# A convolution and ELU feed-forward kernel: first tile in token halves, conv output permuted on its way into PSUM

## Chip, cores, metric

The kernel runs on one core of a Trainium2 chip. The metric is the device time of one execution in microseconds (us); lower is better. It is measured over several runs, and one further execution is profiled. Engines are called by their short names: PE (TensorE, matrix multiply; PEld is its weight load), DVE (VectorE), ACT (ScalarE), POOL (GpSimd), SP (SyncE, here only a DMA queue).

## What is computed

```python
def _attn_ref(x, weight):            # x (8, 4096, 192), weight (8, 7)
    w = softmax(weight, axis=-1)     # with 1e-9 added to the sum
    x_pad = np.concatenate([np.zeros((B, 6, 192)), x], axis=1)
    idx = np.arange(S)[:, None] + np.arange(7)[None, :]
    x_unf = x_pad[:, idx, :].reshape(B, S, 7, 8, 24)
    return np.einsum('hk,bskhg->bshg', w, x_unf).reshape(B, S, 192)

def _moe_ref(x, w_in, w_out):        # w_in (192, 2048), w_out (2048, 192)
    h = x @ w_in
    g = np.where(h > 0.0, h, np.exp(np.minimum(h, 0.0)) - 1.0)
    return g @ w_out
```

A causal convolution of seven taps over the sequence, with one set of taps for each of 8 heads of 24 channels, is followed by a feed-forward layer with ELU, over 8 x 4096 = 32768 tokens.

## The kernel before

The tokens are cut into 32 tiles of 1024 (`SUP`), each into two groups of 512 (`GS`). Channels are split into three blocks j of 64; group 0 uses partitions 0 to 63 of every operand and group 1 partitions 64 to 127. So a matmul has 64 rows of the array, and the two row halves work side by side on the two groups.

For a tile in the steady state:

- *conv* (`c`, L978): eight heads, two row halves: 16 matmuls of 240 columns with band matrices `Tm` as weights over windows of x (`xg`), into a PSUM bank that ACT evacuates to `csb` (L745). A DMA transpose (L597, on SP's queue) makes `att` of it, channels on partitions.
- *h* (`h`, L1003): 16 chunks q of 128 hidden units, two groups: three accumulating matmuls (j = 0, 1, 2) of 512 columns fill one PSUM bank, a unit. There are 1024 units in all.
- *ELU* of a unit: ACT takes exp from PSUM into `E` (L749), POOL clamps E to [0, 1] (L702), DVE computes max(E - 1, h) into `gT` (L865). DVE's combine frees the bank.
- *o* (`o`, L1026): 256 matmuls of 192 columns of `gT` and `w_out` for a tile; ACT evacuates to `osb` (L756), SP writes it out.

The order of PE's instructions is made by a planner in the file when the kernel is built. It keeps a clock for each row half, gives each matmul a duration (`MM_H`, `MM_O`, `MM_C`) and each bank a time at which it is free. For the first 16 steps n (one step is chunk q of tile 0) the function `live` picks what is ready first, from modelled ends of the ELU and from the landing times assumed in `LANDS`; the later steps have fixed places (`O_AT`, `CONV_AT`). Eight banks of PSUM are shared by all kinds of result. The order is fixed: at run time PE executes it in sequence and waits on semaphores.

The first tile doesn't go through `xg`, `Tm` and the DMA transpose. Its path:

- SP loads the weights (L1043) and an 8-token halo `xh` (L1047); ACT loads all 1024 tokens in one DMA (L714, 768 KB), token p*8+i on partition p.
- DVE and ACT make the softmax (L769 to L792, exp at L721), PE spreads it (`s`, L904 and L911), DVE copies it to `wcol` (L799) and multiplies it with the identity into seven diagonal matrices `taps` in one instruction (L801). Two rows of matmuls on zeros (`w`, L900, six and four of them by `WARM`) stand before and after `s`.
- ACT casts x into three channel blocks (L724, three instructions), PE transposes them (`t`, L926; the halo at L937), DVE and ACT evacuate to `xT` (L821, L736).
- PE does the convolution with `taps` (`d`, L954): for j = 0 and 1 five taps of 512 columns, DVE the other two taps (L830, L835, L848); for j = 2 seven taps in two halves of 256, evacuated by ACT and DVE (L740, L850).
- The group 1 copy of `w_in` (partitions 64 to 127) is made from the group 0 rows by ACT (L730, chunk columns 0 to 511, and 1024 to 1279 after unit 6), by DVE (L853, columns 512 to 1023) and by an SP DMA (L1066).

POOL first builds `ones`, `ident`, `owner` and `block8` (L653 to L676), then issues in this order: nine loads of `w_in` (L638; three column chunks, one load for each j, because block j of a head is 8 consecutive rows), the first part of `w_out` (L649), x of tile 1 (L618, two loads), two parts of `w_out`, x of tile 2; then it begins with the clamps. SP also writes the band matrices to DRAM and reads them back shifted as `Tm` (L1049, L1058).

The channel order of `att` in the kernel before is head, j, i (j of 3, i of 8). In the steady state it comes from the way a conv matmul reads x: `"p w (j i) -> p j w i"` over a head's 24 channels (L981), written to PSUM in order.

Of the kernel before, what the change touches and what calls it, by code (L numbers as in the profile page):

```python
# [5 lines left out]
ALU = mybir.AluOpType  # L6
# [31 lines left out]
WARM = (6, 1, 4)  # L38
WCOLS = ((0, 4 * FC), (4 * FC, 8 * FC), (8 * FC, 16 * FC))
WOUT = (0, 4, 8, 16)  # L40
HALO = 8
BW = P
ON_DVE = (2, 2, 0)
XL = GS - CW * (NWIN - 1) + PAD
XI = SUP // P
# [7 lines left out]
LATE_Q, COPY_AT = 10, 6  # L53
LIVE, UNTIL = 16, 16
EARLY_O = (4, 8)
LANDS = {"x": {1: 7200.0, 2: 14200.0}, "w_in": 10200.0, "w_out": (3900.0, 8400.0, 11000.0)}
# [3 lines left out]
TURNS = 260.0  # L60
X_AT = ((2, 1, 1), (1, 1, 0))
ZERO_AT = 8
# [3 lines left out]
def bass_lightweight_conv__then__act_elu_kernel(  # L66
# [41 lines left out]
    conv_half = {}  # L108

# [15 lines left out]
    def modelled():  # L125
        return step[0] < UNTIL
# [9 lines left out]

    def h_items(n, r):
        def issue(j):
            take_bank(("h", n, r), r)
            plan.append((clock[r], ("h", n, r, j)))  # L140
            if j == 2:
                freed[bank_of["h", n, r]] = clock[r] + MM_H + HELD["h"]
                if modelled():
                    elu(n, r, clock[r] + MM_H)

        return [(MM_H, lambda j=j: issue(j), None) for j in range(3)]
# [15 lines left out]
    def o_items(k, g, rt, qs, visit, first, final):  # L162
# [4 lines left out]
        def issue(i):  # L167
            q, kb = todo[i]
            take_bank(("a", k, g), rt)
            if modelled():  # L170
                t = NQ * (k // 2) + q
                clock[rt] = max(clock[rt], gt_at[t, g], turned.get((k, g), 0.0) if first and i == 0 else 0.0)
# [42 lines left out]
    def block_items(n, g, rt):  # L215
        k, b = divmod(n - O_AT[g], NB)
        if k < 1:
            q = n - EARLY_O[g]
            if not 0 <= q < NQ:
                return []  # L220
            items = o_items(0, g, rt, range(q, q + 1), 2 * q + rt, True, True)
            return evacuated(items, 0, g) if q == NQ - 1 and rt == 1 else items
        items = o_items(k, g, rt, range(QB * b, QB * (b + 1)), 2 * b + rt, True, True)
        return evacuated(items, k, g) if b == NB - 1 and rt == 1 else items

    def live(last, convs, turns):
        hq = [list(range(last)) for _ in range(2)]
        cq = [list(convs), list(convs)]
        far = float("inf")

        def h_ready(rt):
# [8 lines left out]
            late = rt == 1 and s == 0 and q >= LATE_Q  # L240
            return max(min(freed), att_at[s], LANDS["w_in"] if late else 0.0)

# [10 lines left out]
        def o_ready(rt, g):  # L253
# [5 lines left out]
            t = max(gt_at.get((NQ * (k // 2) + q, g), far) for q in range(q0, q1))  # L259
# [6 lines left out]
        while any(hq) or any(cq) or any(map(any, turns)):  # L266
            best = None
            for rt in range(2):
# [22 lines left out]
            if what[0] == "h":  # L291
                n = hq[rt].pop(0)
                go(h_items(n, rt))
            elif what[0] == "c":
# [7 lines left out]
            else:  # L302
                g = what[1]
                k, q0, q1, visit = turns[rt][g].pop(0)
                go(o_items(k, g, rt, range(q0, q1), visit, True, True))
# [9 lines left out]
    start_up = [("t", j) for j in (0, 3, 1, 2)] + [("d", j) for j in range(3)]  # L315
    for i, (b, what) in enumerate(
        ((0, ("t", 0)), (3, ("t", 3)), (1, ("t", 1)), (2, ("t", 2)))
        + ((4, ("d", 0)), (5, ("d", 1)), (6, ("d", 2)), (7, ("d", 2)))
    ):
        occupant[b], freed[b] = what, i - 10.0  # L320
        bank_of.setdefault(what, b)
    turns = [[[], []], [[], []]]
    for rt in range(2):
        for g in range(2):
            turns[rt][g] += [(0, q, q + 1, 2 * q + rt) for q in range(LIVE - EARLY_O[g])]
    live(LIVE, [(n, m) for n in range(LIVE) for m in conv_steps.get(n, ())], turns)
    for n in range(LIVE, NP):
        step[0] = n
        if n == UNTIL:
            clock[:] = [max(clock)] * 2  # L330
# [33 lines left out]
    pe_order += [("w", 0, WARM[0]), ("s",), ("w", 0, WARM[2])]  # L364
    for what in start_up:
        pe_order.append(what)
# [3 lines left out]
    for at, item in sorted(plan, key=lambda p: p[0]):  # L370
        if item[0] == "h" and item[3] == 2:
# [3 lines left out]
            act_order.append(item[:3])  # L375
        elif item[0] == "c" and item[2:] == (1, HU - 1):
# [18 lines left out]
    x_before = {}  # L395
    for s in range(2, NS):
# [11 lines left out]
    with ExitStack() as stack:  # L408
# [15 lines left out]
        xs = sbuf("xs", [P, XI, D], FP32)  # L424
        xh = sbuf("xh", [HALO, D], FP32)
        xbh = sbuf("xbh", [HALO, 3, 2, HP], BF16)
        xb = sbuf("xb", [P, 3, XI, HP], BF16)
# [16 lines left out]
        part = sbuf("part", [P, 2, GS], FP32)  # L444
# [10 lines left out]
        s_w = [sema(f"s_w{i}") for i in range(6)]  # L455
        s_wc = sema("s_wc")
        s_sel = sema("s_sel")
# [5 lines left out]
        s_xs = sema("s_xs")  # L463
# [17 lines left out]
        s_wd = sema("s_wd")  # L481
        s_wa = sema("s_wa")
        s_band = sema("s_band")
        s_part = sema("s_part")
# [35 lines left out]
        def att_need(s):  # L520
# [4 lines left out]
            ("t", 0): (0, 1),  # L525
            ("t", 1): (1, 0),
            ("t", 2): (2, 0),
            ("t", 3): (0, 2),
            ("d", 0): (0, 3),
            ("d", 1): (0, 4),  # L530
            ("d", 2): (3, 5),
# [7 lines left out]
        def transposed(j):  # L539
            if j == 3:  # L540
                return xT[:, :, 0:HALO], H[:, bank_of["t", 3], 0 : 3 * HALO].rearrange(
                    "p (j c) -> p j c", j=3
                )
            return xT[:, j, HALO : HALO + GS], H[:, bank_of["t", j], :]

        def first_att(j, c0, c1):
            b = bank_of["d", j] + (j == 2 and c0 > 0)
            return att[:, 0, j, c0:c1], H[:, b, c0:c1]
# [52 lines left out]

        @block.gpsimd
        def _gpsimd(g: bass.BassGpSimd):
# [31 lines left out]
            def load_w_in(k):  # L635
                c0, c1 = WCOLS[k]
                for j in range(3):
                    g.dma_start(  # L638
                        w_in[0:HP, j, c0:c1],
                        bass.AP(  # L640
                            tensor=moe_w_in.tensor,
                            offset=8 * j * FF + c0,
                            ap=[[CPH * FF, HEADS], [FF, 8], [1, c1 - c0]],
                        ),
                    ).then_inc(s_w[k], 16)

            def load_w_out(k):
# [3 lines left out]
                ).then_inc(s_w[3 + k], 16)  # L651
# [11 lines left out]
            ).then_inc(s_id)  # L663
            for step in range(2):
# [20 lines left out]
            load_w_in(0)  # L685
            load_w_in(1)
            load_w_in(2)
            load_w_out(0)
            for gr in range(2):
                load_x(1, gr)  # L690
            load_w_out(1)
            load_w_out(2)
            for gr in range(2):
                load_x(2, gr)
# [17 lines left out]
        def _scalar(a):  # L712
            W = Waits(a)
            a.dma_start(  # L714
                xs[:, :, :], x_flat[0:SUP, :].rearrange("(p i) d -> p i d", i=XI)
            ).then_inc(s_xs, 16)
# [5 lines left out]
            W(s_xs, 16)  # L722
            for j in range(3):
                a.activation(  # L724
                    xb[:, j, :, :].rearrange("p i (h e) -> p (i h) e", e=8),
                    xs[:, :, :].rearrange("p i (h j e) -> p j (i h) e", j=3, e=8)[:, j],
                    ACT.Copy,
                ).then_inc(s_cast)
            def upper_half(c0, c1):
                a.activation(  # L730
                    w_in[HP:P, :, c0:c1], w_in[0:HP, :, c0:c1], ACT.Copy
                ).then_inc(s_wa)

            for j in range(1, 3):
                W(s_xt, j + 2)
                a.activation(*transposed(j), ACT.Copy).then_inc(s_fa)  # L736
            W(s_w[0], 48)
            upper_half(*WCOLS[0])
# [369 lines left out]
```

## Time and profile before

| | us |
|---|---|
| median of 3 runs (lowest, highest) | 723.49 (723.15, 723.59) |
| the profiled execution | 722.73 |
| its span, first to last instruction | 720.8 |
| PE, ACT, POOL, DVE busy in the span | 714.6, 678.6, 670.1, 642.8 |
| mean granted TensorE clock | 1.00 |
| period of a tile in the steady state | 21.85 |

Issues of the first 15 us (start, issue length, landing after issue, us):

| DMA | queue | start | length | landing after |
|---|---|---|---|---|
| wq | SP | 0.80 | 0.41 | wait for it ended at 2.24 |
| xs, 768 KB | ACT | 0.81 | 0.38 | 4.6 |
| w_in, nine | POOL | 2.44 to 7.02 | 0.56 to 0.78 | 3.0 for the first, 6.8 for the last |
| band matrices out | SP | 6.12 | 0.37 | 5.5 |
| w_out, first part | POOL | 7.56 | 0.91 | 7.6 |
| x of tile 1, two | POOL | 8.37, 9.24 | 0.96, 0.95 | 8.1, 10.4 |
| w_out, second, third | POOL | 10.09, 10.83 | 0.85, 0.99 | 10.6, 11.9 |
| Tm | SP | 11.63 | 0.35 | 7.0 |
| x of tile 2, two | POOL | 11.70, 12.56 | 0.97, 0.98 | 12.3, 12.7 |

How to read the views used: a timeline row has the start, the length of the merged stretch, the engine, the line, the operation and tiles, shapes, and in brackets the idle time before it with what ended it. A row by stages has a stretch, its length and the busy time of each engine in it with the number of instructions, then the granted clock, the share of DMA time and the bytes moved. Matmuls are pipelined, so their lengths overlap, and the distance of their starts tells the rate.

### The profile page before, as it was taken

The numbers are of one execution on the slowest core, as the hardware profiler recorded it, in microseconds if no ns is written. First come the engines' busy times: TensorE is split into PE (matmuls) and PEld (weight loads), VectorE is DVE, ScalarE is ACT, GpSimd is POOL, SyncE is SP. The second block draws the span as 40 slices with busy tenths as digits, with TensorE's granted clock in tenths as the row PEclk, the third lists the DMA queues.
The fourth block names the chain that finished last, engine by engine and source line by source line (L and its number), as shares of the span: only waits on it lengthen the run. The fifth ranks groups of instructions, "written<-read, shape, count | busy, mean of one in ns | idle before, by whom it ended". The sixth has DMA issues, their size and how long they took to land.

```text
span 720.8 us, 27612 instructions
## 1 busy us (share of the span) xinstructions
PE 714.6 (99%) x11846; PEld 676.0 (94%) x11847; DVE 642.8 (89%) x1048; ACT 678.6 (94%) x1289; POOL 670.1 (93%) x1115
## 2 busy tenths in 40 slices
PE   8999999999999999999999999999999999999998
PEld 4689999999999999999999999999999999999997
DVE  7989898998899988989888989988989989899994
ACT  6999999999999999999999999999999999999994
POOL 9999999999999999999999999999999999999893
PEclk9999999999999999999999999999999999999999
DMA  9655354554254664344553456552535543645212
GB/s 172 92 87 78 64 90 74 95 87 83 54 96 72 88 97 63 73 83 86 87 97 50 84 74 96 86 86 51 96 73 89 94 69 67 92 79 83 71 35 68
DMA packets 132735, 58.75 MB, mean 82 GB/s; under 512 B 98614, under 2 KB 132036, under 8 KB 132612
## 3 DMA queue, kind: packets, MB, share of 16 engines
q1 hardware_dynamic: 88388, 39.32, 23.9%
q0 software_dynamic: 43936, 16.77, 23.1%
q8 instruction: 93, 1.52, 0.9%
q10 hardware_dynamic: 288, 0.88, 0.4%
q14 instruction: 30, 0.25, 0.1%
HBM read 34.63 MB, written 25.46 MB: 83 GB/s over the span
## 4 chain that ended last, share of the span: by engine, by line
PE 95%; POOL 2%; DVE 1%; ACT 1%; issue 0%; DVEq 0%; POOLq 0%
PE H L1026 54%; PE H L1003 38%; PE H L978 3%; DVE gT L865 1%; POOL w_in L638 1%; ACT E L749 1%; POOL xg L618 0%; POOL w_out L649 0%; ACT csb L745 0%; POOL E L702 0%; POOL owner L666 0%; ACT osb L756 0%; DVE osb L856 0%; POOL block L676 0%; POOL ident L655 0%
## 5 line engine op out<-in xcount | busy, mean ns | idle before, releaser
L865 DVE SCALAR_TENSOR_TENSOR gT<-E,H 128x512 f16<-128x512 f32 x1024 | 633.0, 683 | 64.1 <-POOL E L702 62.4
L1026 PE MATMUL H<-w_out,gT 64*128 64x192 f16 x8192 | 682.2, 243 | 0.1
L1003 PE MATMUL H<-att,w_in 64*128 64x512 bf16 x3072 | 680.3, 376 | 0.6 <-DVE gT L865 0.4
L1026 PEld LDWEIGHTS H<-w_out,gT 64*128 64x128 f16 x8192 | 625.9, 94 | 22.3 <-PE H L1026 1.6
L702 POOL TENSOR_SCALAR E<-E 128x512 f32<-128x512 f32 x1024 | 607.6, 615 | 38.4 <-ACT E L749 28.2
L749 ACT ACTIVATE E<-H 128x512 f32<-128x512 f32 x1024 | 593.1, 602 | 26.5 <-PE H L1003 1.6
L1003 PEld LDWEIGHTS H<-att,w_in 64*128 64x128 bf16 x3072 | 275.2, 93 | 7.9 <-issue 1.2
L978 PE MATMUL H<-xg,Tm 64*128 64x240 bf16 x496 | 91.2, 263 | 0.2 <-DVE gT L865 0.2
L745 ACT ACTIVATE csb<-H 112x480 bf16<-112x480 f32 x124 | 70.1, 565 | 0.1
L756 ACT ACTIVATE osb<-H 128x384 f32<-128x384 f32 (+1 forms) x129 | 62.2, 484 | 6.8 <-PE H L1026 6.8
L618 POOL DMA_DIRECT2D xg<-in_x_dram x62 | 55.4, 898 | 0.2 <-issue 0.2
L978 PEld LDWEIGHTS H<-xg,Tm 64*128 64x128 bf16 x496 | 43.7, 94 | 4.7 <-DVE gT L865 1.1
L856 DVE COPY osb<-H 128x192 f32<-128x192 f32 x1 | 0.4, 358 | 7.3 <-PE H L1026 7.3
L900 PE MATMUL H<-zw 128*128 128x512 bf16 x10 | 4.0, 555 | 1.2 <-DVE zw L764 1.2
L638 POOL DMA_DIRECT2D w_in<-in_moe_w_in_dram x9 | 5.2, 617 | 0.0
L724 ACT ACTIVATE xb<-xs 128x512 bf16<-128x512 f32 x3 | 1.7, 622 | 2.4 <-DMA xs<-in_x_dram 2.4
L954 PE MATMUL H<-xT,taps 128*128 128x256 bf16 (+1 forms) x23 | 3.7, 314 | 0.2 <-issue 0.2
L900 PEld LDWEIGHTS H<-zw 128*128 128x128 bf16 x10 | 1.1, 128 | 2.8 <-issue 1.4
L954 PEld LDWEIGHTS H<-xT,taps 128*128 128x128 bf16 x24 | 2.2, 97 | 1.5
L649 POOL DMA_DIRECT2D w_out<-in_moe_w_out_dram x3 | 2.6, 916 | 0.0
L717 ACT ACT_TABLE_LOAD x1 | 1.3, 1283 | 1.2 <-PEq L1093 1.2
L730 ACT ACTIVATE w_in<-w_in 64x1536 bf16<-64x1536 bf16 (+1 forms) x2 | 2.3, 1164 | 0.0
(43 smaller groups left out, 19.9 us busy)
## 6 DMA issues: line engine op xcount, KB each, us to landing
out_dram<-osb SPq DMA_DIRECT2D x126, 192.0 KB, 3.5
xg<-in_x_dram POOLq DMA_DIRECT2D x61, 240.0 KB, 5.0
xs<-in_x_dram ACTq DMA_DIRECT2D x1, 768.0 KB, 4.6
att<-csb SPq DMA_TRANSPOSE x31, 4.6
w_in<-in_moe_w_in_dram POOLq DMA_DIRECT2D x6, 64.0 KB, 3.0
w_in<-in_moe_w_in_dram POOLq DMA_DIRECT2D x3, 128.0 KB, 5.4
w_out<-in_moe_w_out_dram POOLq DMA_DIRECT2D x2, 192.0 KB, 9.1
w_out<-in_moe_w_out_dram POOLq DMA_DIRECT2D x1, 384.0 KB, 11.9
```

Source lines behind the costliest of these rows:

```text
L618: g.dma_start(xg[0:rows, b, 2 * w0 + gr : 2 * w1 : 2, :], src).then_inc(s_x[b][gr], 16)
L638: g.dma_start(w_in[0:HP, j, c0:c1], bass.AP(tensor=moe_w_in.tensor, offset=8 * j * FF + c0, ap=[[CPH * FF, HEADS], [FF, 8], [1, c1 - c0]], ...
L702: g.tensor_scalar(out=E[:, i % NE, :], in0=E[:, i % NE, :], scalar1=1.0, scalar2=0.0, op0=ALU.min, op1=ALU.max,).then_inc(s_clp)
L745: a.activation(*conv_evac(W, m), ACT.Copy).then_inc(s_ce)
L749: a.activation(E[:, i % NE, :], H[:, bank_of[item], :], ACT.Exp).then_inc(s_exp)
L756: a.activation(*out_evac(W, *item[1:]), ACT.Copy).then_inc(s_oev[item[2]])
L865: v.scalar_tensor_tensor(out=gT[:, s % NG3, q, u, :], in0=E[:, i % NE, :], scalar=1.0, in1=H[:, bank_of[item], :], op0=ALU.subtract, op1=A ...
L900: pe.matmul(H[:, bank, :], zw[:, 0:P], zw[:, 0:GS], start=True, stop=True)
L954: ins = pe.matmul(H[:, bank_of[item] + half, c0:c1], taps[:, tap, :], xT[:, j, HALO - PAD + tap + c0 : HALO - PAD + tap + c1], start=(tap ...
L978: ins = pe.matmul(H[:, bank_of["c", m], 256 * q : 256 * q + UC], Tm[rows, h, :], xg[rows, s % NXB, :, CPH * h : CPH * (h + 1)].rearrange(" ...
L1003: ins = pe.matmul(H[:, bank_of[item[:3]], :], w_in[HP * r : HP * (r + 1), j, FC * q : FC * (q + 1)], att[HP * r : HP * (r + 1), s % 2, j, ...
L1026: ins = pe.matmul(acc_of(k, g)[:, D * kb : D * (kb + 1)], gT[HP * rt : HP * (rt + 1), t % NG3, q, g, t0 : t0 + P], w_out[HP * rt : HP * (r ...
```

## The change

It has these parts:

- **Channel order.** `att` gets the order head, i, j: channel 3p + j is on partition p of block j. `w_in` then loads with three consecutive rows for each partition, all three j in one DMA, in four column chunks (`NCH`). A conv matmul reads x in memory order and writes its 240 columns to PSUM at the places that ACT's evacuation reads as before.
- **x of tile 0** comes in four loads of 64 partitions x 4 tokens: half 0 (the first 256 tokens of each group) and half 1, group 0 on SP, group 1 on ACT; the halo is loaded on ACT's queue between its two.
- **First tile in halves.** One cast, three transposes `t` of 256 tokens, three convolutions `d` with all seven taps on PE for half 0; the same for half 1 as `T` (before the first h) and `D` (placed by `JOBS` after two, two and three steps). The DVE part of the convolution is gone. The first 8 steps (`SPLIT`) compute two chunks q of 256 tokens in one bank, six matmuls of 256 columns, half 0 in steps 0 to 3 and half 1 in steps 4 to 7.
- **POOL's order.** The first `w_in` load goes between `ident` and `owner`, w_out's second part ahead of x of tile 1; x of tile 2 is issued before the first clamp through `X2_AT`.
- **Smaller ones.** `taps` is made in seven instructions; the xbh cast stands ahead of `wcol`; four `w` matmuls after `s` become one, behind `t3`; group 1's `w_in` columns 0 to 1023 are copied by DVE; the early o blocks are laid out anew (`BEGUN`, `LATER`), and so are the planner's landing times.

```diff
-WARM = (6, 1, 4)
-WCOLS = ((0, 4 * FC), (4 * FC, 8 * FC), (8 * FC, 16 * FC))
+WARM = (6, 1, 1)
+NCH = 4
+LATE_Q, COPY_AT = 10, 8
+SPLIT = 8
-LATE_Q, COPY_AT = 10, 6
-LIVE, UNTIL = 16, 16
-EARLY_O = (4, 8)
-LANDS = {"x": {1: 7200.0, 2: 14200.0}, "w_in": 10200.0, "w_out": (3900.0, 8400.0, 11000.0)}
+LIVE = 16
+BEGUN = (6, 5)
+LATER = ((16, 18), (16, 18, 20))
+LANDS = {"x": {1: 8400.0, 2: 14000.0}, "w_in": 11500.0, "w_out": (2600.0, 5400.0, 9000.0)}
+JOBS = ((2, ("D", 0, 0)), (2, ("D", 0, 1)), (3, ("D", 1, 2)))
+X2_AT = (0, 0)
...
-    start_up = [("t", j) for j in (0, 3, 1, 2)] + [("d", j) for j in range(3)]
+    start_up = [("t", 3), ("w", 0, WARM[2]), ("t", 0), ("t", 1), ("t", 2)]
+    start_up += [("d", j) for j in range(3)] + [("T", 0), ("T", 1)]
...
+        def load_first(eng, half, gr):
+            eng.dma_start(
+                xs[HP * gr : HP * (gr + 1), XI * half : XI * (half + 1), :].rearrange(
+                    "p i d -> p (i d)"
+                ),
+                bass.AP(
+                    tensor=x_flat.tensor,
+                    offset=(GS * gr + GH * half) * D,
+                    ap=[[XI * D, HP], [1, XI * D]],
+                ),
+            ).then_inc(s_xs[half][gr], 16)
...
             def load_w_in(k):
-                c0, c1 = WCOLS[k]
-                for j in range(3):
-                    g.dma_start(
-                        w_in[0:HP, j, c0:c1],
...
+                c0, c1 = FF // NCH * k, FF // NCH * (k + 1)
+                g.dma_start(
+                    w_in[0:HP, :, c0:c1],
+                    bass.AP(
+                        tensor=moe_w_in.tensor,
+                        offset=c0,
+                        ap=[[3 * FF, HP], [FF, 3], [1, c1 - c0]],
+                    ),
+                ).then_inc(s_w[k], 16)
...
             ).then_inc(s_id)
+            load_w_in(0)
             for step in range(2):
...
-            load_w_in(0)
             load_w_in(1)
             load_w_in(2)
+            load_w_in(3)
             load_w_out(0)
+            load_w_out(1)
             for gr in range(2):
                 load_x(1, gr)
-            load_w_out(1)
             load_w_out(2)
-            for gr in range(2):
-                load_x(2, gr)
...
-            a.dma_start(
-                xs[:, :, :], x_flat[0:SUP, :].rearrange("(p i) d -> p i d", i=XI)
-            ).then_inc(s_xs, 16)
+            load_first(a, 0, 1)
+            a.dma_start(xh[:, :], x_flat[GS - HALO : GS, :]).then_inc(s_xh, 16)
+            load_first(a, 1, 1)
...
+            cast(0)
             for j in range(3):
...
+                a.activation(*first_evac(("t", j)), ACT.Copy).then_inc(s_fa)
+            cast(1)
+            for j in (0, 2):
+                W(s_first, j + 1)
+                a.activation(*first_evac(("d", j)), ACT.Copy).then_inc(s_fa)
...
+            upper_half(0)
+            W(s_first, 2)
+            v.tensor_copy(*first_evac(("d", 1))).then_inc(s_fd)
             for j in range(2):
+                W(s_xt, 5 + j)
+                v.tensor_copy(*first_evac(("T", j))).then_inc(s_fd)
+            upper_half(1)
...
                     ins = pe.matmul(
-                        H[:, bank_of["c", m], 256 * q : 256 * q + UC],
+                        H[:, bank_of["c", m], 256 * q : 256 * q + UC].rearrange(
+                            "p (j w i) -> p w i j", j=3, i=8
+                        ),
                         Tm[rows, h, :],
                         xg[rows, s % NXB, :, CPH * h : CPH * (h + 1)].rearrange(
-                            "p w (j i) -> p j w i", j=3
+                            "p w (i j) -> p w i j", j=3
                         ),
...
...
-            sy.dma_start(xh[:, :], x_flat[GS - HALO : GS, :]).then_inc(s_xh, 16)
-            W(s_tap, 3)
+            for half in range(2):
+                load_first(sy, half, 0)
+            W(s_tap, KSIZE + 2)
```

## The prediction

> **What bounds the kernel now.** I read the stages first (busy time of each engine per stretch), then the timeline of the first 20 us, then the conv rows, then the groups of instructions. Stages; columns are stretch, length, busy us of PE, PEld, DVE, ACT, POOL, granted clock, DMA share, GB/s:
>
> ```profile
> 15.00:20.00 5.00, 4.88 (x41) 2.50 (x43) 5.00 (x9) 4.95 (x10) 4.79 (x9) 1.00 1.40 244
> 20.00:25.00 5.00, 5.00 (x65) 3.43 (x61) 5.00 (x9) 4.88 (x11) 4.58 (x9) 1.00 1.13 135
> 60.00:80.00 20.00, 20.00 (x341) 19.39 (x338) 18.64 (x31) 19.22 (x38) 18.95 (x33) 1.00 0.57 88
> ```
>
> From 60 us on PE is never idle and the other engines are: the steady state is PE's. Before that, PE's matmuls come sparsely and DVE, ACT and POOL are full. By starts, 15 to 40 us holds 110 matmuls of L1003, 140 of L1026, 24 of L978; at 216, 82.5 and 102.5 ns each (512, 192 and 240 columns at their spacing) and two row halves side by side that is 11.9+5.8+1.2 = 18.9 us of work in 25: 6.1 us free. The same count for 60 to 85 us fills it. So until about 40 us the ELU chain (ACT exp, POOL clamp, DVE combine) sets the pace, and the end moves by as much as that chain's start moves, while PE's extra work fits in the 6.1 us.
>
> The timeline (start, length, engine, line):
>
> ```profile
> 0.81 0.38 ACTq L714 DMA_DIRECT2D xs<-in_x_dram  x1
> 2.44 5.22 POOL L638 DMA_DIRECT2D w_in<-in_moe_w_in_dram  x9
> 5.40 1.67 ACT L724 ACTIVATE xb<-xs 128x512 bf16<-128x512 f32 x3 [2.35 <-DMA xs<-in_x_dram]
> 8.05 3.66 PE L954 MATMUL H<-xT,taps 128*128 128x512 bf16 x23 [0.16 <-issue]
> 11.70 1.83 POOL L618 DMA_DIRECT2D xg<-in_x_dram  x2
> 12.73 3.54 ACT L749 ACTIVATE E<-H 128x512 f32<-128x512 f32 x7 [0.60 <-PE H L1003]
> 13.44 4.19 POOL L702 TENSOR_SCALAR E<-E 128x512 f32<-128x512 f32 x7
> 14.22 7.93 DVE L865 SCALAR_TENSOR_TENSOR gT<-E,H 128x512 f16<-128x512 f32 x13 [1.03 <-POOL E L702]
> ```
>
> Two things end together at 13.44 us: the first tile (x lands 5.40, h starts 11.64, first exp 12.73) and POOL's row of DMA issues. Both must move for a gain.
>
> **POOL's issues.** Nine w_in issues, 2.44 to 7.56, become four of 192 runs. Issues of 64 runs start 0.55 apart, w_out's of 512 runs 0.81, x's of 640 runs 0.87; by the straight line between the first two I take 0.63, ends 0.55 and 0.87. So 4 x 0.63 = 2.5 for 5.1: 2.5 saved (1.6 to 2.9). The rest only changes order: w_out's second load passes x(1), and x(2) still stands before the first clamp. First clamp free at 13.44 - 2.5 = 11.0 (10.6 to 11.9). The first w_in issue now precedes owner and block: block ends at 3.2 instead of 2.5, and wnb, which reads it, starts at 3.90.
>
> **The x half.** 768 KB took 4.6 us; wq, 0.2 KB, ended its wait 1.44 after issue, so bytes cost 3.15 and half of them 1.6. SP's load leaves behind wq at 1.27: 1.27+1.44+1.6 = 4.3, and w_in's first load now runs beside it; I take 4.4, ends 3.8 and 5.9 (1.6 more if w_in takes half the rate). ACT's three issues, 0.3 each beyond the first, push the exp table and softmax back 0.6: wnb 4.5, the wcol copy 5.1, the xbh cast (0.35) hidden in that wait. The single multiply of 1.09 becomes seven of about 0.2 (nearest rows: 128x56 in 0.19, 128x256 in 0.42): taps from 5.5 to 6.9, wband 7.1 instead of 6.1.
>
> Cast of 768 elements: 1.5 x 0.53 = 0.8, done 5.2. Eight transposes, then an evacuation of 0.38 (L740's size): the first ends 6.1. d is 21 matmuls of 256 columns, which start 0.109 apart in L954's row: 2.3, ending 8.5 with a pause for taps. ACT's second cast waits for the second x half; behind it stand the evacuations of d0 and d2, and behind d on PE stand T0 and T1, before the first h. Cast to about 7.7, T to 9.2, h0 at 9.3 (11.64 before). Six matmuls of 256 columns in two row halves 0.65, then the 0.2 from matmul to ACT: exp 10.15; clamp possible 0.71 after (the old distance): 10.85. POOL at 11.0 still ends last. **Gain 2.4.** DVE's d1, T0, T1 evacuations (0.4+0.7+0.4) and two weight copies (1.0 each) end before its first combine at 11.7, down from 14.22.
>
> **The second half.** D is 21 x 0.109 = 2.3 us of PE, in the 6.1 free. The step from L954 (128*128) to L1003 (64*128) was 0.20 instead of 0.11; six such steps 0.6, in the same cover, at full price if PE were full. [...] D's evacuations cost ACT 0.53+0.38 = 0.9, behind which exps wait; ACT is nearly full until 40 us, but runs ahead while POOL still issues. I take 0.3 on the path, ends 0 and 0.9. Whole-tile h, later o blocks and the tail keep their counts: nothing.
>
> Behind the conv on PE everything waits for Tm. The band write leaves 1.0 later, and 5.5+7.0 of landing put Tm at 19.6 (18.6 before), while the conv of tile 1 would come 2.4 earlier than 20.5: up to 1.5 us of PE, covered by the eight banks that the ELU chain still holds (8 x 0.6 = 4.8); 1.5 if that cover is gone.
>
> **The conv matmuls.** 496 of them run in the steady state, where nothing covers:
>
> ```profile
> 20.51 0.26 PE L978 MATMUL H<-xg,Tm 64*128 64x240 bf16 x1
> 20.61 0.26 PE L978 MATMUL H<-xg,Tm 64*128 64x240 bf16 x1
> 6.09 0.63 PE L926 MATMUL H<-ident,xb 64*64 64x64 bf16 x16 [0.45 <-ACT xb L724]
> ```
>
> They start 0.10 apart for 240 columns: already the column rate of the other rows, so reading x in order gains nothing. What is new is writing PSUM 80 words apart. The nearest row is L926, which writes every eighth word: 16 matmuls in 0.63, less the last one's 0.24, are 26 ns each, 52 per pair; each also loads its own 64 columns of weights, so 64 loaded plus 64 streamed columns account for it with no cost for the step. The same 52 ns would also fit 64 columns written at half rate behind a hidden load. So 0 to 100 ns each; I take 0, since the load must cost something.
>
> [...]
>
> **Sum.** 2.4 - 0.3 = 2.1 earlier. The profiled execution took 722.73 (span 720.8), 0.76 under the median of 723.49; span 718.7, time 720.6 for it, and 721.4 for the median. With the ends above, 720.3 (2.7 gained, and half a us from earlier w_out) to 722.9.
>
> **Rivals.** *PSUM at half rate*: 496 x 100 ns, two row halves side by side: 24.8 longer, less 2.1: 746. For it: L926's 52 ns, and PE's full stages. Against: the weight loads explain the same row. It decides from 2100/248 = 8.5 ns per matmul on.
>
> *The clock comes late*: the six first zw matmuls take 0.63 apiece, the last of the four later ones 0.38. Three of those four go, and softmax's delay leaves PE idle from 4.0 to 4.9. If the array stays slow, d takes 2.3 more, h0 comes at 11.6, the first clamp at 13.2: 723.4, no change. Against: the granted clock reads 1.00 in every stretch, and transposes and d fill PE from 5.2.
>
> *Tile 1 gets late*: the conv's x(1) landed at 19.7, with DMA engines nine tenths busy to 25 us, and now w_out's second load is ahead of it. If it lands one such load (1.0) later than before, the conv moves to 20.7, att(1) from 30.5 to 30.7, and h of tile 1, due 2.1 earlier, starves: the gain is gone and up to 1 is lost, 724.5. Against: w_in's issues no longer pace the queue.
>
> **How the numbers follow.** Forecast 0.58, late clock 0.15, late tile 0.09, half rate 0.18. About 0.2% (1.4 us) is what a measurement tells from no change. Forecast under 722.0: 0.85 of 0.58, so faster 0.50; the rest of it and most of the late clock, same 0.21; the others, slower 0.29. Its own range is 720.3 to 722.9; with the two late rivals 719.8 to 726.5, which leaves out the half rate.
>
> **What would show it.** First h near 9.3, POOL's first clamp near 11.0, first combine near 11.7; conv matmuls still 0.10 apart; a tile period of 21.85 us. Wrong if the period grows (PSUM), if d's matmuls start 0.2 apart (clock), if the first clamp waits for ACT (x), or if a gap before the conv or tile 1's h exceeds 1.5 us.

## The result, and the profile after

The changed kernel takes 746.95 us (median of 4 runs, 746.78 to 748.25), the kernel before 723.4 on the same chip: a ratio of 1.033, interval 1.0312 to 1.0348, so 3.3% slower. The profiled execution took 746.78, its span is 744.9 (before 720.8). The forecast was 721.4, with a range up to 722.9; the rival *PSUM at half rate* had worked out 746.

Where nearly all of the 24.1 us of span went is seen in one row. First the groups of instructions, line, engine, operation, shape and count, then busy us and mean ns of one, for the kernel before:

```profile
L978 PE MATMUL H<-xg,Tm 64*128 64x240 bf16 x496 | 91.2, 263 | 0.2 <-DVE gT L865 0.2
```

and for the changed one:

```profile
L1034 PE MATMUL H<-xg,Tm 64*128 64x240 bf16 x496 | 141.3, 386 | 0.5 <-DVE gT L910 0.2
L799 ACT ACTIVATE csb<-H 112x480 bf16<-112x480 f32 x124 | 69.9, 564 | 0.6 <-PE H L1034 0.6
```

The same 496 matmuls of the same shape last 123 ns longer each. ACT's evacuation of what they write takes 0.564 us, as long as in e5 below, which writes PSUM in order. Two of them that follow each other in one row half, at their start, from the timeline (start, length):

```profile
22.75 0.36 PE L1034 MATMUL H<-xg,Tm 64*128 64x240 bf16 x1
22.90 0.41 PE L1034 MATMUL H<-xg,Tm 64*128 64x240 bf16 x1
```

They start 0.15 apart instead of 0.10. The stages (stretch, length, busy us of PE, PEld, DVE, ACT, POOL with counts, granted clock, DMA share, GB/s):

```profile
15.00:20.00 5.00, 5.00 (x81) 4.13 (x81) 3.99 (x7) 4.03 (x8) 3.52 (x7) 1.00 1.46 233
60.00:80.00 20.00, 20.00 (x332) 19.42 (x329) 17.76 (x29) 18.58 (x36) 18.62 (x32) 1.00 0.47 78
```

From 60 to 80 us PE is as full as before but does 332 matmuls instead of 341, and every other engine has less to do. Spread over the 31 tiles that go through the conv, 24.1 us is at most 0.78 a tile (a part of it is the first tile's): a period of about 22.6 instead of 21.85. In the early stages DVE and POOL, full before (5.00 and 4.79 from 15 to 20 us), now have gaps.

The first tile, which should have brought 2.1 us, brought nothing. Its timeline (start, length; in brackets the idle time before and what ended it):

```profile
0.80 0.55 ACTq L648 DMA_DIRECT2D xs<-in_x_dram  x1
...
1.39 0.95 ACTq L770 DMA_DIRECT2D xh<-in_x_dram  x1
...
2.37 0.49 ACTq L648 DMA_DIRECT2D xs<-in_x_dram  x1
...
2.89 1.28 ACT L772 ACT_TABLE_LOAD   x1 [2.89 <-issue]
...
4.88 0.84 ACT L781 ACTIVATE xb<-xs 128x768 bf16<-128x768 f32 x1 [0.16 <-DMA xs<-in_x_dram]
...
5.77 0.16 PE L949 MATMUL H<-wn,owner 8*128 8x7 bf16 x1 [1.78 <-DVE wnb L854]
...
6.75 1.49 PE L986 MATMUL H<-ident,xb 64*64 64x64 bf16 x24
...
8.17 3.07 PE L1009 MATMUL H<-xT,taps 128*128 128x256 bf16 x21
...
11.18 0.87 PE L986 MATMUL H<-ident,xb 64*64 64x64 bf16 x24
...
11.98 1.48 PE L1072 MATMUL H<-att,w_in 64*128 64x256 bf16 x24
...
13.54 2.34 POOL L757 TENSOR_SCALAR E<-E 128x512 f32<-128x512 f32 x4 [2.33 <-ACT E L803]
...
14.18 2.48 DVE L910 SCALAR_TENSOR_TENSOR gT<-E,H 128x512 f16<-128x512 f32 x4 [0.57 <-POOL E L757]
```

The first h comes at 11.98 (11.64 before), the first clamp at 13.54 (13.44), the first combine at 14.18 (14.22). POOL is free at 11.21, 2.2 earlier than its 13.44 before and near the forecast of 11.0, and then waits 2.33 for ACT's exp. The reader should also see PE idle for 1.78 until softmax's spread at 5.77, and 24 transposes of one shape taking 1.49 the first time (half 0) and 0.87 the second (half 1).

### The profile page after: what moved, and what is told of

It is laid out like the page before. It is cut to its first block, busy times and chain, and to the rows that moved or that the text cites. A ratio compares the mean times of both kernels' runs of the same rounds, so it can differ in the third digit from the quotient of the medians.

```text
span 744.9 us, 27742 instructions
## 1 busy us (share of the span) xinstructions
PE 738.2 (99%) x11910; PEld 706.1 (95%) x11910; DVE 651.5 (87%) x1050; ACT 681.1 (91%) x1291; POOL 670.6 (90%) x1110
## 3 DMA queue, kind: packets, MB, share of 16 engines
q1 hardware_dynamic: 88532, 39.71, 22.6%
## 4 chain that ended last, share of the span: by engine, by line
PE 98%; ACT 1%; DVE 0%; ACTq 0%; issue 0%; POOL 0%; DVEq 0%
PE H L1095 54%; PE H L1072 35%; PE H L1034 8%; PE H L1009 1%; PE H L986 0%; DVE gT L910 0%; ACT L772 0%; ACT E L803 0%; ACT csb L799 0%; ACTq L648 0%; ACTq L770 0%; POOL E L757 0%; PE H L945 0%; DVE xbh L862 0%; DVE osb L894 0%
## 5 line engine op out<-in xcount | busy, mean ns | idle before, releaser
L910 DVE SCALAR_TENSOR_TENSOR gT<-E,H 128x512 f16<-128x512 f32 x1024 | 644.3, 684 | 77.0 <-POOL E L757 73.1
L1095 PE MATMUL H<-w_out,gT 64*128 64x192 f16 x8192 | 690.9, 244 | 0.2
L1072 PE MATMUL H<-att,w_in 64*128 64x512 bf16 (+1 forms) x3120 | 687.8, 373 | 0.2 <-ACT csb L799 0.2
L1095 PEld LDWEIGHTS H<-w_out,gT 64*128 64x128 f16 x8192 | 656.1, 96 | 21.1 <-PE H L1095 1.8
L1072 PEld LDWEIGHTS H<-att,w_in 64*128 64x128 bf16 x3120 | 278.3, 93 | 4.2 <-DVE gT L910 1.0
L1034 PE MATMUL H<-xg,Tm 64*128 64x240 bf16 x496 | 141.3, 386 | 0.5 <-DVE gT L910 0.2
L799 ACT ACTIVATE csb<-H 112x480 bf16<-112x480 f32 x124 | 69.9, 564 | 0.6 <-PE H L1034 0.6
L1034 PEld LDWEIGHTS H<-xg,Tm 64*128 64x128 bf16 x496 | 41.1, 93 | 3.3 <-PE H L1034 1.6
L1009 PE MATMUL H<-xT,taps 128*128 128x256 bf16 x42 | 5.7, 293 | 0.0
L1009 PEld LDWEIGHTS H<-xT,taps 128*128 128x128 bf16 x42 | 4.1, 104 | 1.3 <-issue 0.6
```

The costliest lines, as they stand in the source:

```text
L799: a.activation(*conv_evac(W, m), ACT.Copy).then_inc(s_ce)
L910: v.scalar_tensor_tensor(out=to, in0=e, scalar=1.0, in1=h, op0=ALU.subtract, op1=ALU.max,).then_inc(s_tt)
L1009: ins = pe.matmul(H[:, bank_of[item[:2]], p0 : p0 + GH], taps[:, tap, :], xT[:, j, c0 + tap : c0 + tap + GH], start=(tap == 0 and (not hal ...
L1034: ins = pe.matmul(H[:, bank_of["c", m], 256 * q : 256 * q + UC].rearrange("p (j w i) -> p w i j", j=3, i=8), Tm[rows, h, :], xg[rows, s % ...
L1072: ins = pe.matmul(H[:, bank_of[item[:3]], c0 : c0 + t1 - t0], w_in[HP * r : HP * (r + 1), j, FC * q : FC * (q + 1)], att[HP * r : HP * (r ...
L1095: ins = pe.matmul(acc_of(k, g)[:, D * kb : D * (kb + 1)], gT[HP * rt : HP * (rt + 1), t % NG3, q, g, t0 : t0 + P], w_out[HP * rt : HP * (r ...
```

## Experiments on the conv matmuls

Each was timed beside the kernel before on the same chip; on the three chips used that kernel's medians were 723.3 to 723.5. The edits of e1 to e4 touch only the conv matmul's two patterns (L1034), on the changed kernel unless said; e5 also moves a pattern on ACT. A pair below is one conv matmul in each of the two row halves: there are 248.

**e1**, written in order, with x read in the order that this needs:

```diff
-  H[:, bank_of["c", m], 256 * q : 256 * q + UC].rearrange("p (j w i) -> p w i j", j=3, i=8),
+  H[:, bank_of["c", m], 256 * q : 256 * q + UC],
...
-  "p w (i j) -> p w i j", j=3
+  "p w (i j) -> p j w i", j=3
```

> The changed kernel with one edit: a conv matmul reads x in the order j, w, i (steps of 3 channels inside a head, 6 bytes) and writes its 240 columns to PSUM one after the other. Channel order, loads and first tile stay those of the changed kernel. Theory (scattered PSUM writes cost the 24 us): conv matmuls go back from 386 to about 263 ns, the tile period from 22.6 to 21.85 us, and the time to 722 to 724, which is also what the new first tile is worth by itself. Rival (the cost sits in the first tile, the o blocks laid out anew, or elsewhere): the time stays near 747. Second rival (a scattered read costs as much as a scattered write): between 735 and 747.

738.26 us, ratio 1.0203 (1.0188 to 1.0219). Only a part of the loss went, in the range of the second rival; the matmuls last 329 ns:

```profile
L1034 PE MATMUL H<-xg,Tm 64*128 64x240 bf16 x496 | 122.6, 329 | 0.5 <-DVE gT L910 0.2
```

The write is in order here, so what is left is the read: it takes every third channel, steps of 6 bytes, where the kernel before read runs of eight channels.

**e2**, x in memory order as in the change, but written in runs of two words, the next run 80 words away:

```diff
-  "p (j w i) -> p w i j", j=3, i=8
+  "p (j r b) -> p r j b", j=3, b=2
...
-  "p w (i j) -> p w i j", j=3
+  "p w (x j b) -> p w x j b", j=3, b=2
```

> The changed kernel with x still read in memory order, but the 240 columns written to PSUM in runs of two neighbouring words, the next run 80 words away. The channels of tiles 1 to 31 come out in another order than the reference's; the amount of work is the same. [...] Rival (each jump of the address costs, whatever the run): half as many jumps, half the cost, about 735. Rival (any pattern that is not contiguous costs in full): 747.

724.24 us, ratio 1.0009 (1.0000 to 1.0019), and the matmuls last what they did before:

```profile
L1034 PE MATMUL H<-xg,Tm 64*128 64x240 bf16 x496 | 91.3, 263 | 0.5 <-DVE gT L910 0.2
```

Against the change this differs only in writing two adjacent words before it jumps: 746.95 - 724.24 = 22.7 us, or 92 ns for each of the 248 pairs of matmuls. The jump itself costs nothing; single words do.

**e3**, written in runs of eight words, read in steps of 6 bytes that stay inside the 48 bytes of one head's channels:

```diff
-  "p (j w i) -> p w i j", j=3, i=8
+  "p (j w i) -> p w j i", j=3, i=8
...
-  "p w (i j) -> p w i j", j=3
+  "p w (i j) -> p w j i", j=3
```

> The changed kernel with x read in the order w, j, i and written to PSUM in runs of eight words, 80 words apart; the result is the reference's. [...] Cost for each jump: an eighth of the jumps, about 726. Any pattern that is not contiguous: 747.

729.04 us, ratio 1.0077 (1.0062 to 1.0092), matmuls of 287 ns. Neither expectation was met. If writing in runs of eight costs no more than in runs of two (taken, not tried by itself), 729.04 - 724.24 = 4.8 us is the read: steps of 6 bytes again, though cheaper than in e1, where the same step runs through all ten windows before the next j.

**e4**, the kernel before with single-word writes and reads in steps of 16 bytes:

```diff
-  H[:, bank_of["c", m], 256 * q : 256 * q + UC],
+  H[:, bank_of["c", m], 256 * q : 256 * q + UC].rearrange("p (j w i) -> p w i j", j=3, i=8),
...
-  "p w (j i) -> p j w i", j=3
+  "p w (j i) -> p w i j", j=3
```

> The kernel before with the write alone: its conv matmuls iterate w, i, j, so every word lands 80 words from the last; x is read with steps of 8 channels (16 bytes). Nothing of the first tile is touched. Theory: the whole loss of 24 us comes with this one edit, 747 to 749, tile period 22.6. Rival (the loss needs the new first tile): 723.4. If a read in steps of 16 bytes costs too, more than 750.

756.23 us, ratio 1.0455 (1.0437 to 1.0472), matmuls of 396 ns: 32.8 us slower. The first tile is untouched here, so the loss belongs to the patterns alone. It is some 10 us more than the 22.7 of the single-word write; the read in steps of 16 bytes is what else differs, but it was not run by itself.

**e5**, the conv reads and writes in order, and ACT's evacuation (L799) picks the channels out of PSUM in steps of three words:

```diff
...
-  .rearrange("p h (r i) -> p h r i", i=8),
+  .rearrange("p h (w i j) -> p h j w i", i=8, j=3),
...
-  H[:, bank_of["c", m], 256 * q : 256 * q + UC].rearrange("p (j w i) -> p w i j", j=3, i=8),
+  H[:, bank_of["c", m], 256 * q : 256 * q + UC],
...
-  xg[rows, s % NXB, :, CPH * h : CPH * (h + 1)].rearrange("p w (i j) -> p w i j", j=3),
+  xg[rows, s % NXB, :, CPH * h : CPH * (h + 1)],
```

> The changed kernel with the permutation moved to ACT: a conv matmul reads x in memory order and writes PSUM in order, and the evacuation to csb reads PSUM in steps of three words. The result is the reference's. Theory (only TensorE's scattered words are dear): conv matmuls 263 ns, csb evacuation still 0.565, 723.8 to 724.7, the same as with runs of two, so that the new first tile is worth about nothing or slightly less (forecast had been 2.1 us gained). Rival (ACT pays for a scattered read of PSUM): csb evacuation over 0.7, ACT over 21.8 us a tile, 727 or more.

724.53 us, ratio 1.0018 (1.0009 to 1.0027); matmuls of 263 ns, the evacuation unchanged at 564 ns. So the permutation is free on ACT, and this kernel is the new first tile by itself: it costs 1.1 us where 2.1 were to be gained. All that follows builds on this kernel.

## Experiments on the first tile

**e6**, softmax ahead: ACT issues one x load, then does the exp table and softmax's exp, then issues the second; the halo goes on SP's queue between its two.

```diff
   load_first(a, 0, 1)
-  a.dma_start(xh[:, :], x_flat[GS - HALO : GS, :]).then_inc(s_xh, 16)
-  load_first(a, 1, 1)
...
   a.activation(wex[:], wq2[:], ACT.Exp).then_inc(s_wex)
+  load_first(a, 1, 1)
...
-  for half in range(2):
-      load_first(sy, half, 0)
+  load_first(sy, 0, 0)
+  sy.dma_start(xh[:, :], x_flat[GS - HALO : GS, :]).then_inc(s_xh, 16)
+  load_first(sy, 1, 0)
```

> e5_act_permutes with the loads issued elsewhere: ACT issues one x load ahead of its exp table load and the other behind the softmax exp; the halo goes to SP, between its two x loads. Theory A (ACT's three issues, 2.1 us, hold up softmax, and softmax holds up taps, transposes and the clock): softmax exp near 2.9 instead of 4.5, h0 at 10.5 to 11 instead of 12, first clamp about 1.2 us earlier, 722.4 to 723.2. Theory B (the cold array alone sets h0): no gain, h0 within 0.3 us. Theory C (x's landing sets it): no gain, the cast waits for the load.

724.66 us, ratio 1.0020 (1.0011 to 1.0029). Softmax's spread did come at 4.30 instead of 5.77, and PE then stood still for the halo instead; from the timeline:

```profile
4.30 0.16 PE L948 MATMUL H<-wn,owner 8*128 8x7 bf16 x1 [0.31 <-DVE wnb L853]
...
5.52 0.47 DVE L861 CAST xbh<-xh 8x192 bf16<-8x192 f32 x1 [1.37 <-DMA xh<-in_x_dram]
...
6.75 1.49 PE L985 MATMUL H<-ident,xb 64*64 64x64 bf16 x24
```

The 6 KB halo, issued at 1.88 behind a 192 KB load, landed 3.6 later. One wait took the other's place: the transposes start at the same 6.75.

**e7**, ten matmuls on zeros before softmax's spread instead of six, to keep PE busy through its wait:

```diff
-WARM = (6, 1, 1)
+WARM = (10, 1, 1)
```

> e5_act_permutes with ten instead of six matmuls on zeros ahead of softmax's, which fill PE's idle time from 4.0 to 5.7 us; nothing else. Theory B (the cold array holds up h0): transposes start 0.053 a pair instead of 0.104, d's matmuls 0.109 instead of 0.214 from the first on, h0 1.4 us earlier, first clamp about 1.3 earlier, 722.3 to 723.1. Theory A (softmax behind ACT's issues alone): no gain.

723.01 us, ratio 0.9994 (0.9985 to 1.0002): 1.5 better than e5, and level with the kernel before. Timeline:

```profile
1.25 3.76 PE L945 MATMUL H<-zw 128*128 128x512 bf16 x10 [1.25 <-DVE zw L826]
...
6.53 0.87 PE L986 MATMUL H<-ident,xb 64*64 64x64 bf16 x24
...
7.43 2.48 PE L1009 MATMUL H<-xT,taps 128*128 128x256 bf16 x21
...
10.64 1.48 PE L1068 MATMUL H<-att,w_in 64*128 64x256 bf16 x24
...
12.21 2.34 POOL L757 TENSOR_SCALAR E<-E 128x512 f32<-128x512 f32 x4 [1.19 <-ACT E L803]
15.25 1.19 POOL L757 TENSOR_SCALAR E<-E 128x512 f32<-128x512 f32 x2 [0.70 <-ACT E L803]
16.92 1.36 POOL L757 TENSOR_SCALAR E<-E 128x512 f32<-128x512 f32 x2 [0.49 <-ACT E L803]
```

Work was added and the time fell: the transposes take 0.87 instead of 1.49, the first convolution 2.48 instead of 3.60 in e5's profile (3.07 in the changed kernel's), the first clamp comes 1.87 earlier than e5's 14.08. So the array was slow in the changed kernel, though the granted clock reads 1.00 in all its rows. The changed kernel's first convolution (8.17, 3.07 above) shows both speeds. Two stretches of 1 us in it, with the busy us of PE and PEld for L1009 alone, counts, clock, DMA share and GB/s:

```profile
8.36:9.36 1.00, 1.00 (x6) 0.75 (x5) 1.00 1.14 151
9.60:10.60 1.00, 1.00 (x12) 0.89 (x10) 1.00 1.20 174
```

Six matmuls in one, twelve in the other, and the clock column says 1.00 for both. In the first it is no measurement: a row subtracts only recorded losses, and the clock records in these traces begin where the matmuls become fast. They begin at 9.44 us in the changed kernel and at 10.53 in e5, just where the convolution's matmuls go from 0.21 to 0.11 apart, and at 4.18 in e7 and 4.85 in the kernel before.

The last two lines of e7's timeline show what is still lost: behind four clamps POOL waits 0.70 for ACT's exp, behind two more 0.49. A longer wait, 0.88 before the clamp at 19.93, comes behind ACT's own copy of w_in (L809, 0.84 from 18.39); no variant here moved that copy.

**e8**, e6 with four such matmuls behind the halo's transposes instead of one:

```diff
-WARM = (6, 1, 1)
+WARM = (6, 1, 4)
```

> e6_softmax_first with four instead of one matmul on zeros between the halo's transpose and t0. If A and B both hold and what they give adds up, h0 near 9.5 as forecast, first clamp 11.2 to 11.5 (POOL's issues), 721 to 722, under the kernel before. If PE is warm in e6_softmax_first already, the same as e6_softmax_first or 0.3 more, since four matmuls stand ahead of t0.

725.20 us, ratio 1.0016 (1.0006 to 1.0026). In the profile the first clamp came at 12.86, better than e5 and 0.65 worse than e7, which is what the four matmuls on zeros behind the halo take more than e7's one there (1.04 for 0.39). The array was fast early in that execution (its clock records begin at 4.39), so the slow array is not what is left. The eleven times spread from 723.03 to 726.23, where e7's lie within 0.6.

**e9**, e7 with the halo first on ACT's queue, ahead of x, then one x load, softmax's exp, the other x load (nine and three matmuls on zeros):

```diff
-  load_first(a, 0, 1)
   a.dma_start(xh[:, :], x_flat[GS - HALO : GS, :]).then_inc(s_xh, 16)
-  load_first(a, 1, 1)
+  load_first(a, 0, 1)
...
   a.activation(wex[:], wq2[:], ACT.Exp).then_inc(s_wex)
+  load_first(a, 1, 1)
```

> The ten-warm kernel (ACT permutes, ten matmuls on zeros before softmax's spread) with ACT's queue in another order: the halo first, then x of half 0, then the exp table and softmax's exp, and only then x of half 1; nine matmuls on zeros before softmax's spread and three behind the halo's transposes. If the first tile is late because softmax stands behind three issues and the halo lands behind a large load, both come 1 to 1.5 us earlier, the transposes wait for the cast alone (end 5.9 instead of a start at 6.53), the first h comes at 10.0 instead of 10.64 and the time falls from 723.0 to about 722.5. If x itself sets the pace (its landing, or the halo in front of it costs what it gains), h stays at 10.6 and the time at 723.0 within 0.3.

724.46 us, ratio 1.0013 (1.0005 to 1.0022), a miss. Softmax and halo were ready earlier (spread at 5.12, the halo's transposes at 5.19), but x wasn't:

```profile
6.54 0.84 ACT L781 ACTIVATE xb<-xs 128x768 bf16<-128x768 f32 x1 [2.71 <-DMA xs<-in_x_dram]
...
7.43 0.87 PE L986 MATMUL H<-ident,xb 64*64 64x64 bf16 x24 [1.28 <-ACT xb L781]
```

The x load was issued at 1.43 instead of 0.80, and the cast found both loads landed at 6.54 instead of 5.04: 0.63 later in the queue became 1.5 later on arrival.

**e12**, e7 with only the last ACT load moved: x of half 1 behind softmax's exp.

```diff
   load_first(a, 0, 1)
   a.dma_start(xh[:, :], x_flat[GS - HALO : GS, :]).then_inc(s_xh, 16)
-  load_first(a, 1, 1)
...
   a.activation(wex[:], wq2[:], ACT.Exp).then_inc(s_wex)
+  load_first(a, 1, 1)
```

> The ten-warm kernel with one move on ACT's queue: x of half 1 is issued behind softmax's exp instead of ahead of the exp table; x of half 0 and the halo stay first. The 0.49 us of that issue no longer stands before softmax: its exp ends at 4.2 instead of 4.71, the spread starts at 5.3 instead of 5.76, and the transposes wait for the cast alone (5.9 to 6.0 instead of 6.53), so the first h is at 10.1 to 10.2 and the first clamp at 11.7. By the step from the kernel with six to that with ten matmuls on zeros (first clamp 1.87 earlier, end 1.5 earlier) the end comes 0.4 earlier: 722.6. If the halo's landing sets the pace, nothing before 6.5 moves and the time is 723.0 within 0.3; if x of half 1, issued at 4.2, comes too late for the second cast at 7.9, the time is above 723.3.

726.31 us, ratio 1.0039 (1.0023 to 1.0055). The first part came as expected (transposes at 6.20), the third outcome decided:

```profile
3.91 0.48 ACTq L648 DMA_DIRECT2D xs<-in_x_dram  x1
...
6.20 0.87 PE L986 MATMUL H<-ident,xb 64*64 64x64 bf16 x24
...
11.06 0.84 ACT L781 ACTIVATE xb<-xs 128x768 bf16<-128x768 f32 x1 [3.45 <-DMA xs<-in_x_dram]
...
12.76 2.74 PE L1068 MATMUL H<-att,w_in 64*128 64x256 bf16 x24
```

Issued at 3.91, after w_in's first loads, 192 KB of x landed 7.1 later, and the first h, behind the second cast's transposes, comes at 12.76 and is slow again (2.74 for what took 1.48). Here the clock was recorded; stretches of all engines, the granted clock third from the end:

```profile
12.00:13.00 1.00, 1.00 (x28) 0.86 (x30) 0.35 (x1) 0.45 (x2) 0.00 (x0) 0.88 1.24 285
13.00:14.00 1.00, 1.00 (x12) 0.71 (x10) 0.97 (x3) 0.00 (x0) 0.00 (x0) 0.50 1.52 207
16.00:17.00 1.00, 1.00 (x11) 0.84 (x9) 1.00 (x3) 0.62 (x2) 0.93 (x3) 0.91 1.52 180
```

At 0.50 until it rises again, the 0.88 puts the drop at 12.76 and the 0.91 its end at 16.18: 3.42 us at half speed, behind 2.28 us in which PE stood idle for x. The nine times go with the mean clock of their executions: 724.4 to 724.8 at 1.000, 726.2 to 726.6 at 0.998, 728.0 and 729.2 at 0.995. By that, late x without a drop cost 1.5 us against e7, and the drops the rest.

**e10**, e7 with one tap instead of seven in the convolution of half 1:

```diff
-  for tap in range(KSIZE):
+  for tap in range(1 if half else KSIZE):
```

> The ten-warm kernel with one tap instead of seven in the convolution of half 1 of the first tile (the second 256 tokens of each group of the first 1024 tokens then come out wrong): 18 matmuls of 0.109 us, 1.96 us of PE, go from the stage in which PE was taken to have 6 us free. If that cover holds, at most the forecast's 0.3 us is gained: 722.7 to 723.0. If the stage has no cover, because the ELU chain starves while PE makes half 1, the time falls by 1 to 2 us, to 721.0 to 722.0, and POOL's waits of 0.70 and 0.49 us between its first clamps shrink.

722.18 us, ratio 0.9982 (0.9973 to 0.9991): 0.8 less than e7 for 1.96 us of PE work, between the two expectations. (Its profiled execution had a fast array only from 6.99, so its first clamp is 0.32 later than e7's.) POOL then runs seven clamps in a row before its first wait:

```profile
12.53 4.30 POOL L757 TENSOR_SCALAR E<-E 128x512 f32<-128x512 f32 x7 [1.50 <-ACT E L803]
17.23 1.19 POOL L757 TENSOR_SCALAR E<-E 128x512 f32<-128x512 f32 x2 [0.41 <-ACT E L803]
```

**e11**, e7 with the second of the three convolutions of half 1 one step later:

```diff
-JOBS = ((2, ("D", 0, 0)), (2, ("D", 0, 1)), (3, ("D", 1, 2)))
+JOBS = ((2, ("D", 0, 0)), (3, ("D", 0, 1)), (3, ("D", 1, 2)))
```

> The ten-warm kernel with the convolutions of half 1 apart: block 0 after two steps, blocks 1 and 2 after three (before: blocks 0 and 1 after two, block 2 after three). The third step's h is then due 0.76 us earlier on PE. If the ELU chain's gaps there (POOL 0.70 and 0.49 us) are what the first tile's head start is lost to, the first of them goes and the second grows by less; the time falls by 0.3 to 0.7, to 722.3 to 722.7. If the gaps only move, or PE's own work sets the end, 723.0 within 0.3.

723.00 us, ratio 0.9994 (0.9985 to 1.0003), no change against e7:

```profile
12.21 3.50 POOL L757 TENSOR_SCALAR E<-E 128x512 f32<-128x512 f32 x6 [1.11 <-ACT E L803]
16.92 1.28 POOL L757 TENSOR_SCALAR E<-E 128x512 f32<-128x512 f32 x2 [1.21 <-ACT E L803]
```

The two waits of 0.70 and 0.49 have become one of 1.21, and the seventh clamp starts at 16.92 in both. The starvation has only moved.

## Why the prediction was wrong

**The step that failed: the conv matmuls.** "So 0 to 100 ns each; I take 0, since the load must cost something." It is 92 ns each with the two row halves side by side (22.7 us over 248 pairs), near the top of the bounds. The bounds held, the choice inside them did not. L926's 52 ns a pair fitted two readings, weight load or half-rate write, and the argument for the first (the load must cost something) didn't exclude the second. The conv's own rows spoke against it: each of L978's 496 matmuls has a weight load of 128 columns (0.09 us in PEld's rows), and they still start 0.10 apart, so a load can be hidden. Whether L926's row, with loads of 64 columns, is the load's or the write's was not tried, and stays open. What the runs show of the write: pairs of words 320 bytes apart cost nothing (e2, 263 ns as before), single words make a matmul last 123 ns longer (386).

**Reading x in order gains nothing:** right as far as it went, since the read before was free (e5 and before have 263 ns). But that was the runs of eight channels. The read isn't free in every order: e1, with the write in order, shows it (329 ns), and e3 and e4 fit (287 and 396).

**The first tile: the sum's 2.1 us were also wrong**, and would have left the time at 724.5 had the conv cost nothing (e5). The first h was forecast at 9.3 and came at 11.98. The 2.7 between split by rows: the transposes start at 6.75 instead of 5.2 (1.55), they and the first evacuation take 1.42 instead of 0.9 (0.5), the convolution 3.0 instead of 2.4 (0.6), the rest 0.8 as forecast. e7 bears the split out: with a fast array the first h comes at 10.64, and the 1.34 that are left over 9.3 are the transposes' start (6.53 for 5.2).

- *"ACT's three issues, 0.3 each beyond the first, push the exp table and softmax back 0.6"*: mis-sized. Their starts are 0.59, 0.98 and 0.52 apart, and the exp table starts 1.67 later than before (2.89 for 1.22). The 0.3 was read from the short issues of the kernel before, where the halo's took 0.28 on SP; on ACT it takes 0.95, while SP issues two loads and POOL one.
- *The halo* was forecast to hide behind softmax. It does, but as e6 shows only just: with softmax earlier, it is the halo that is waited for, and then x (e9).
- *The clock.* The rival named the mechanism (the matmuls on zeros cut, PE idle through softmax's delay) and gave it 0.15. It happened, with a longer idle time (1.78 for 0.9), and e7 shows it: filling that wait gave 1.5 us. The argument against it was the granted clock of 1.00, which stands in the rows only because these traces have no clock record before the array is fast: in the kernel before the records begin at 4.85, behind the six matmuls of 0.63 that the rival itself points to. The array was fast 2.9 us after PE's first matmul in e7, 3.6 in the kernel before and 8.2 in the changed kernel (1.25 to 9.44). PE's work alone doesn't set that moment: e6 and e8 give PE the same work up to 6.2 us, yet their profiled executions became fast at 9.34 and 4.39, and e8's times spread by 3.2 us. What sets it was not found.
- *"The second half ... in the 6.1 free"*: right in kind, too generous. Of 1.96 us of PE work, 0.8 shows at the end (e10). A second reading agrees: e7's first clamp is 1.23 earlier than that of the kernel before and its time only 0.4 shorter; e9's is 0.33 earlier (13.11) and its time 1.1 longer. So 0.8 to 1.4 us are lost behind the first clamp, where the forecast had 0.3 (ends 0 and 0.9). PE has the free time, but not where this work stands: the third step's h waits behind it, and the ELU chain, which sets the pace there, runs dry for 0.7 and 0.5 us, and for another 0.9 behind ACT's copy of w_in. Cutting the wait at one place moves it to the next (e11). So "the end moves by as much as that chain's start moves" did not hold either.

**Right:** POOL's row of issues (free at 11.2, forecast 11.0); x's landing nearly (4.4 forecast, the cast starts at 4.88); and of the rival the mechanism and the time, though not its terms: 24.8 less 2.1 was forecast, 22.7 for the conv and 0.8 to 1.1 for the first tile were measured. That the rival's 746 comes so near to 746.95 is in part luck, since the two errors cancel.

The forecast's range was also drawn too narrow by its own terms. With x landing at its late end of 5.9, the first clamp moves from 10.85 to 12.35 and, with the second half's late end of 0.9, the time is 723.3 and not 722.9. The 719.8 and 726.5 given with the two late rivals are not worked out.

The rival *Tile 1 gets late* wasn't told apart: tile 1's conv begins at 22.75 instead of 20.5, but behind a first tile that was late itself, with the read of Tm issued at 14.12 (11.63 before).

No version here that does the whole work beats the kernel before by more than a measurement can tell. e7 and e11 come nearest, 0.4 us under it, with intervals that take in 1.

## What to carry to other kernels

By these runs, a matmul in a stage where PE is full should write PSUM in runs of at least two words (263 ns in e2, 386 with single words) and read its moving operand in runs (263 ns with runs of eight channels in the kernel before, 329 in steps of 6 bytes in e1); where a permutation is needed, it was free on the engine that evacuates the bank (e5, 564 ns with and without). When a row admits two readings and the step is multiplied by 496, the bounds belong in the forecast, and a kernel with one such matmul is worth more than an argument. At the start of a kernel a shorter load is no gain by itself: each DMA issue on ACT pushed back ACT's own work (the three starts 0.59 and 0.98 apart, the exp table 0.52 behind the last), and a place in the issue order counted more on arrival than in the queue (0.63 against 1.5 in e9; e12). And whether the array is fast is read from the distance of the matmuls' starts (here 0.21 or 0.11 for 256 columns) until the trace has its first clock record.

## What the hardware showed that was not expected

- The moving operand's order matters too. Steps of 6 bytes cost 18 ns a pair (e3, 729.04 - 724.53 over 248, if its write is free) or 55 ns (e1, 738.26 - 724.53), by the order of the outer loops. Why the two differ was not found.
- The issue of one and the same load isn't one price: the halo's took 0.28 on SP in the kernel before, 0.46 on SP in e6, 0.58 as the first on ACT in e9, and 0.95 on ACT in the changed kernel while both other queues issued.
- A load's place among the others mattered more here than its size: 192 KB issued at 0.80 and 1.26 were in by 5.04 (e7), with ACT's one moved from 0.80 to 1.43 by 6.54 (e9), and issued at 3.91 by 11.06 (e12), while the 768 KB of the kernel before, issued at 0.81, were in by 5.40.
- PE's idle 2.28 us in the middle of the first tile were followed by a drop to half speed that lasted 3.42 us (e12), and it began only 0.81 after PE had work again (11.95 to 12.76).
